# Block-sparse attention and a two-layer MLP: dense masked attention replaced by attention on gathered key and value blocks

## The chip, the cores and the metric

The kernel runs on one core of a Trainium2 chip. The metric is the device time of one execution in microseconds (us). Of the kernel before, three runs were timed; their median is 1000.07 us.

## The reference

Attention over 4 batches, 8 heads, 768 positions and head size 64, with a mask by blocks of 32 positions (24 blocks). A query block sees its neighbours, itself, the first and the last block, and three sampled blocks; the first and the last query block see everything. The result, as 3072 tokens of 512 numbers, goes through two weight matrices with a gate between them.

```python
    scores = scale * np.matmul(q, k.transpose(0, 1, 3, 2))
    mask = np.abs(blk_i - blk_j) <= window
    mask = mask | (blk_i == 0) | (blk_j == 0) | (blk_i == n_blocks - 1) | (blk_j == n_blocks - 1)
    for qb in range(n_blocks):
        for kb in sampled_blocks[qb]:
            mask[qb * block:(qb + 1) * block, kb * block:(kb + 1) * block] = True
    scores = np.where(mask, scores, -1000000000.0)
    scores = scores - np.max(scores, axis=-1, keepdims=True)
    attn = np.exp(scores)
    attn = attn / (np.sum(attn, axis=-1, keepdims=True) + 1e-09)
    return np.matmul(attn, v).astype(np.float32)
...
    h = x @ w_in
    relu6 = np.clip(h + 3.0, 0.0, 6.0)
    g = h * relu6 / 6.0
    return (g @ w_out).astype(np.float32)
```

The weights arrive as float64 and the sampled blocks as int64; both are read as pairs of 32-bit words. The inner size of the MLP is 2048.

## The kernel before

**Attention.** A unit (class `Unit`, L539) is one batch, one head and one half of the queries (384): 64 units. All 768 keys are used. To keep float32 accuracy with matmuls in the rounded format fp32r, `qh`, `ql`, `kh`, `kl` (L611 to L626) split queries and keys into a rounded high part and a low part that lie above each other on the 128 partitions. `m` (L630) makes a first product of 6 matmuls only to find the row maxima, which `r` and `fin` (L639, L645) reduce by key blocks with the mask added; `s` (L663) makes the scores a second time, keys on the output's partitions, with 12 matmuls of 384 columns, of which 6 add mask and maximum through extra rows (`KB`, `QB`). `e` is the exponential, `av` (L688) the product with the values in plain float32: from unit 12 on 6 matmuls, each on one 64-column half of the array. `suma` to `sumc` and `dm` (L722) make the denominators, which go through DRAM to be inverted and spread (`rg`, `rc`, `rs`, `rb`). `ux` (L761) splits the result into high and low parts.

**MLP.** A step (class `Step`, L774) is one unit of 384 tokens and 256 of the 2048 inner columns: 8 token units of 8 steps, 64 steps. `h` (L823) issues 24 matmuls of 384 columns in fp32r (high by high, low by high, high by low), `ga`, `gb`, `gh`, `gl` make the gate and its two parts on ACT, DVE, ACT and POOL, and `o` (L850) issues 18 matmuls of 512 columns into three PSUM banks that collect over the 8 steps. Low parts of the weights lie in DRAM and are loaded for each step. `oc` and `od` copy and store an output tile.

**Weights.** 32 chunks of 128 x 512 (class `Weight`, L491) are loaded as words (`load`), turned into float32 by `size` and `bits`, and split by `high` and `low`.

**Order.** Every engine runs its instructions in the order in which `SCORE` (L41) names them: `u11 s_0` is operation `s(0)` of unit 11, `m` a step, `w` a weight chunk, `k0` the masks. All DMAs are issued by SP, in that order, so one that waits holds those behind it. PSUM has two tiles of two banks named `big` in turn, one bank `av`, three banks `out`. `k0 warm` issues matmuls without use while TensorE has nothing else. Nearly all instructions have line L359, that of the helper which records them.

Of the kernel before, what the change touches and what calls it, by code (L numbers as in the profile page):

```python
# [17 lines left out]
P = 128  # L21
# [3 lines left out]
HALF = S // 2  # L25
NC = S // P
# [5 lines left out]
NT = HALF // P  # L32
NEG = -1000000000.0


WIDE = 12
BYDMA = 10
QUICK = "0 1 2 3 4 5 6 7 8 9 10 11 12 13 14 15 16 17 18 19 20 21 22 23 24 25 26 27 28 29 30 31"
DIRECT = "0 1 2 3"
COMPACT = "1 3 5 7 9 11"  # L40
SCORE = """  # L41
    u0 loadq loadk; k0 samp table ind ident; u0 loadv; w0 load; w2 load; u1 loadv; u0 qh qb ql kh; k0 index; u1 loadq;
    k0 allow_0 allow_1 warm_09 warm_11; u0 m_0; k0 allow_2; u0 m_1; k0 allow_3 indc; u0 r_0; k0 mq kb_0; w0 size; u0
    r_1; k0 rows; w2 size; k0 identc mqc; u0 kl m_2; k0 qb_00; u0 r_2; k0 qb_11; u1 qh qb; w0 bits_0; u1 loadk; k0
    qb_01; w0 bits_1; k0 qb_10; w0 bits_2; u0 fin_0; w0 high; w1 load; k0 kb_1; u0 fin_1; k0 warm_29 warm_39; u0 mt
    qm; w0 low; k0 warm_41; u0 s_0; u1 ql; w0 save; u0 s_1; w2 bits_0; u2 loadq; u0 e_0; w2 bits_1; u1 kh; u0 av_0; w2
    bits_2; u0 e_1; u1 kl; w3 load; u1 m_0; w2 high; u0 s_2; u1 r_0; w1 size; u0 av_1; w2 low; u2 loadk; u0 e_2; w1
    bits_0; w2 save; u2 qh; u1 m_1; w1 bits_1; u0 av_2; u2 qb; w1 bits_2; u1 r_1; w1 high; w5 load; u2 loadv; w3 size;
    w1 low; k0 warm_52; u1 m_2; u0 dw; u2 ql; w1 save; u0 uc; u1 r_2; u3 loadq; u2 kh; u1 fin_0; k0 warm_68; u2 m_0;
    u1 fin_1; u2 kl; u1 mt; u2 r_0; u1 qm; k0 warm_71; u1 s_0; w5 size; u2 m_1; w3 bits_0; u3 loadk; u1 e_0 s_1; w5  # L50
    bits_0 bits_1; u1 s_2 e_1; w5 bits_2; u1 av_0 e_2; u2 r_1; w4 load; w5 high; w3 bits_1; u2 m_2; u3 qh; u1 av_1; w5
    low; u3 qb; u2 r_2; w5 save; u3 kh; u1 av_2; u3 ql; u2 fin_0; u4 loadq; u3 m_0; u2 fin_1; u3 kl; u1 dw; u3 loadv;
    u2 mt; u3 r_0; u2 qm; w4 size; k0 warm_81; u2 s_0; u1 uc; w4 bits_0; u3 m_1; u4 loadk; u2 s_1 e_0; u1 rg; w3
    bits_2; u3 r_1; w6 load; w3 high; u2 s_2; m1 loadout_0; u2 e_1 av_0; w4 bits_1; u2 e_2; w3 low; u3 m_2; w4 bits_2;
    u4 qh; w3 save; u2 av_1; u4 qb; u3 r_2; w7 load; w4 high; u2 av_2; u3 fin_0; u4 kh ql; u1 rc; u5 loadq; u4 kl; u3
    fin_1; w6 size; u1 rs; u3 mt; u4 m_0 loadv; u3 qm; u4 r_0; u2 uc; u3 s_0; u2 dw; u5 loadk; u3 s_1; w6 bits_0; u3
    e_0; w6 bits_1; u4 m_1; u3 e_1 s_2; w6 bits_2; u3 av_0; u4 r_1; w8 load; w6 high; u3 e_2; w6 low; u1 rb; u4 m_2;
    u5 qh; w4 low; u3 av_1; w6 save; u5 qb; u4 r_2; w4 save; w7 size; u3 av_2; u5 kh; u4 fin_0; u5 ql; u4 fin_1; u5
    kl; u6 loadq; u5 m_0; u3 uc; u5 loadv; u4 mt; u5 r_0; u3 dw; u4 qm; u3 rg; k0 warm_93; u5 m_1; w7 bits_0; w8 size;
    u4 s_0; u6 loadk; w7 bits_1; m1 loadin_1; u4 s_1; m1 loadin_0; w8 bits_0; u4 e_0; w8 bits_1; u4 e_1 s_2; w8  # L60
    bits_2; u4 av_0; u5 r_1; u4 e_2; w10 load; u6 qh; u1 ux_0; u5 m_2; u6 qb; u4 av_1; u6 ql; u1 ux_1; u5 r_2; u7
    loadq; u6 kh; u4 av_2; u5 fin_0; w8 high; u1 ux_2; u5 fin_1; u6 kl; u3 rc; u5 mt; u3 rs; u6 m_0; u4 uc; u6 loadv;
    u5 qm; u6 r_0; w10 size; k0 warm_101; u5 s_0; u7 loadk; w7 bits_2; u4 dw; u5 s_1 e_0; w10 bits_0; w9 load; u6 m_1;
    w10 bits_1; u5 e_1 s_2; u6 r_1; u5 av_0; w7 high; w10 bits_2; u5 e_2; u3 rb; w8 low; u6 m_2; u7 qh; u5 av_1; u6
    r_2; w8 save; u7 qb; w11 load; u7 kh; u6 fin_0; u5 av_2; u7 ql; w10 high; u6 fin_1; u7 kl; u8 loadq; w9 size; u7
    m_0 loadv; u5 uc; u6 mt; u7 r_0; u6 qm; u5 dw; u8 loadk; k0 warm_111; u6 s_0; w9 bits_0; u5 rg; w7 low; u6 s_1
    e_0; u3 ux_0; w7 save; u7 m_1; u6 e_1 s_2; w10 low; u6 av_0; u3 ux_1; w9 bits_1; w10 save; u6 e_2; w9 bits_2; u6
    av_1; u8 qh; u7 r_1; w12 load; u8 qb kh; u3 ux_2; u6 av_2; u8 ql; w9 high; m1 loadout_1; u5 rc; u8 kl; u5 rs; w11
    size; u7 m_2; u9 loadq; u8 loadv; u6 uc; u7 r_2; u6 dw; u9 loadk; u7 fin_0; k0 warm_124; u8 m_0; u7 fin_1; w11
    bits_0; u7 mt qm; u8 r_0; w12 size; k0 warm_131; u7 s_0; w9 low; u8 m_1; u7 e_0 s_1; w11 bits_1; w9 save; u5 rb;  # L70
    u7 s_2; u8 r_1; u7 e_1 av_0; w11 bits_2; u7 e_2; w12 bits_0; w14 load; u9 kh; u8 m_2; w12 bits_1; u7 av_1; u9 qh;
    u8 r_2; u9 kl qb; w11 high; u7 av_2; u8 fin_0; u10 loadk; u8 fin_1; u9 ql; u8 mt; u7 uc; u9 loadv; w11 low; u8 qm;
    u9 m_0; u10 loadq; u7 dw; u9 m_1 r_0; w11 save; w14 size; u7 rg; u9 r_1; k0 warm_142; u8 s_0; u5 ux_0; u8 e_0 s_1;
    w12 bits_2; u5 ux_1; u8 s_2; w14 bits_0; w16 load; u8 e_1 av_0; u5 ux_2; u10 kh; w14 bits_1; u9 m_2; w14 bits_2;
    u8 e_2 av_1; u9 r_2; u10 kl; w18 load; u10 qh qb; u7 rc; u8 av_2; u7 rs; w12 high; w14 high; u9 fin_0; u11 loadk;
    u9 fin_1; u10 ql; u9 mt; u8 uc; u10 loadv; w12 low; u10 m_0; u11 loadq; u9 qm; u8 dw; u9 s_0; u10 r_0; w12 save;
    w16 size; w14 low; u9 s_1 e_0; w16 bits_0; w14 save; u9 e_1 s_2; w16 bits_1; u7 rb; u9 av_0; w18 size; w16 bits_2;
    u9 e_2; w18 bits_0; w13 load; w18 bits_1; u10 m_1; u11 kh; u10 m_2; w18 bits_2; u9 av_1; u11 qh; u10 r_1; u11 kl;
    w15 load; w18 high; u9 av_2; u11 qb; u10 r_2; w16 high; w18 low; u12 loadk; u9 uc; u11 loadv; u7 ux_0; w18 save;
# [858 lines left out]
```

## Time and profile before

| | us |
|---|---|
| timed runs | 1004.21, 1000.07, 997.81 |
| median | 1000.07 |
| profiled execution, first to last instruction (span) | 995.7 |
| TensorE matmul busy (PE) | 961.6 |
| VectorE (DVE) busy | 639.3 |
| ScalarE (ACT) busy | 471.5 |
| GpSimd (POOL) busy | 250.3 |

The profile shows one execution. The page gives its span and no separate time for what lies around it; the median of the timed runs is 4.4 us above the span. PE stands for matmuls, PEld for the weight loads that run beside them, SPq for SyncE as the issuer of DMAs. A float32 matmul is recorded as two instructions, an fp32r matmul as one. A matmul's recorded duration contains its latency, so a stream of them is read from start to start, and the last column of the timeline counts merged instructions.

### The profile page before, as it was taken

The page shows a single profiled execution, that of the slowest core. Times are in us where ns is not written, and L with a number is a line of the kernel's source. Part 1 is how long each engine was busy: PE and PEld are TensorE (multiplying, and loading weights), DVE is VectorE, ACT ScalarE, POOL GpSimd, SP SyncE. Part 2 cuts the span into 40 slices and gives each one's busy share as a digit, 9 for nine tenths or more (in the row PEclk, how much of TensorE's full clock was granted, in tenths as well). Part 3 has the DMA queues.
Part 4 walks back from the last instruction along what each step waited for, and adds up shares of the span by engine and source line. Part 5 has one row for each costly group of instructions (what it writes and reads, how often), then busy time and mean ns, then how long its engine had stood idle before and what let it go on. Part 6 is the DMA issues. An engine that isn't in the chain of part 4 may idle for free.

```text
span 995.7 us, 13391 instructions
## 1 busy us (share of the span) xinstructions
PE 961.6 (97%) x4821; PEld 780.2 (78%) x4821; DVE 639.3 (64%) x900; ACT 471.5 (47%) x712; POOL 250.3 (25%) x149
## 2 busy tenths in 40 slices
PE   8888999999999999999999999999999999999997
PEld 7666776788687888878878778887888777878886
DVE  5787898976767655676666674665766675752111
ACT  5786756563435344444453454444354443432121
POOL 3221222223314122222322233122222213302221
PEclk8999999999999999999999999999999999999999
DMA  6676887665444454435444455454543444414442
GB/s 197 202 240 183 259 290 246 191 213 163 135 131 137 134 154 144 151 103 162 151 144 140 122 161 166 123 158 127 176 147 108 147 131 139 144 49 146 140 119 72
DMA packets 103702, 155.49 MB, mean 156 GB/s; under 512 B 32819, under 2 KB 51891, under 8 KB 103636
## 3 DMA queue, kind: packets, MB, share of 16 engines
q1 hardware_dynamic: 103636, 154.64, 51.1%
q8 instruction: 38, 0.62, 0.3%
q14 instruction: 28, 0.23, 0.1%
HBM read 139.63 MB, written 14.78 MB: 155 GB/s over the span
## 4 chain that ended last, share of the span: by engine, by line
PE 82%; DVE 10%; ACT 2%; DMA 2%; issue 2%; POOL 0%; SPq 0%; DVEq 0%; ACTq 0%
PE big L359 44%; PE out L359 26%; PE av L359 12%; DVE bm L359 3%; DVE xhl L359 2%; DVE acc L359 2%; DVE QA L359 2%; ACT pr L359 1%; DMA wout_lo<-xhl 1%; DMA wraw<-w_out 1%; ACT xhl L359 1%; DMA win_lo<-xhl 0%; DVE wraw L359 0%; ACT qb L359 0%; DVE uu L359 0%
## 5 line engine op out<-in xcount | busy, mean ns | idle before, releaser
L359 PE MATMUL big<-xhl,win_hi 128*128 128x384 f32 x1024 | 264.7, 340 | 0.7 <-DVE bm L359 0.7
L359 POOL TENSOR_TENSOR glo<-g,ghi 128x768 fp32r<-128x768 f32 x64 | 119.8, 1873 | 432.0 <-ACT ghi L359 420.6
L359 ACT ACTIVATE pr<-big 128x768 f32<-128x768 f32 x192 | 153.1, 809 | 101.6 <-PE big L359 100.9
L359 POOL TENSOR_TENSOR kb<-kraw,KA 64x768 fp32r<-64x768 f32 x64 | 124.5, 1945 | 299.6 <-ACT KA L359 242.1
L359 PEld LDWEIGHTS big<-xhl,win_hi 128*128 128x128 f32 x1024 | 184.5, 188 | 14.1 <-issue 7.3
L359 DVE TENSOR_REDUCE bm<-big 128x24 f32<-128x768 f32 x168 | 158.2, 953 | 55.9 <-PE big L359 54.3
L359 PE MATMUL big<-xhl,wlo_in 128*128 128x384 f32 x512 | 172.5, 337 | 0.0
L359 PE MATMUL av<-pr,vo 128*64 128x384 f32 (+1 forms) x768 | 162.7, 493 | 0.2 <-ACT pr L359 0.2
L359 PE MATMUL out<-wout_hi,ghi 128*128 128x512 f32 x384 | 153.3, 399 | 4.7 <-DVE wraw L359 4.7
L359 PE MATMUL out<-wout_hi,glo 128*128 128x512 f32 x384 | 152.1, 396 | 0.0
L359 PE MATMUL out<-wlo_out,ghi 128*128 128x512 f32 x384 | 150.4, 392 | 0.0
L359 PE MATMUL big<-QA,KA 128*128 128x384 f32 x384 | 137.1, 357 | 2.2 <-DVE bm L359 0.8
L359 PE MATMUL big<-qb,kb 97*128 97x384 f32 x384 | 131.2, 342 | 0.6 <-ACT qb L359 0.4
L359 DVE SCALAR_TENSOR_TENSOR g<-g,big 128x768 f32<-128x768 f32 x64 | 60.8, 950 | 110.7 <-ACT g L359 110.4
L359 ACT ACTIVATE g<-big,half_b 128x768 f32<-128x768 f32 x64 | 57.7, 901 | 144.6 <-PE big L359 129.0
L359 PEld LDWEIGHTS av<-pr,vo 128*64 128x64 f32 (+1 forms) x768 | 67.0, 146 | 65.3 <-issue 49.4
L359 PE MATMUL big<-KA,QA 128*128 128x384 f32 x336 | 92.3, 366 | 9.0 <-DVE QA L359 4.1
L359 PEld LDWEIGHTS big<-KA,QA 128*128 128x128 f32 x336 | 74.5, 255 | 31.6 <-issue 8.6
L359 DVE TENSOR_TENSOR acc<-pr 128x768 f32<-128x768 f32 x52 | 54.2, 1042 | 68.2 <-ACT pr L359 68.0
L359 PEld LDWEIGHTS big<-xhl,wlo_in 128*128 128x128 f32 x512 | 96.2, 188 | 0.0
L359 PEld LDWEIGHTS big<-QA,KA 128*128 128x128 f32 x384 | 73.2, 191 | 21.7 <-ACT pr L359 6.1
L359 ACT CAST ghi<-g 128x768 fp32r<-128x768 f32 x64 | 53.3, 833 | 73.4 <-DVE g L359 50.9
(66 smaller groups left out, 1005.3 us busy)
## 6 DMA issues: line engine op xcount, KB each, us to landing
wlo_out<-wout_lo SPq DMA_DIRECT2D x126, 256.0 KB, 2.9
wlo_in<-win_lo SPq DMA_DIRECT2D x126, 256.0 KB, 2.9
kraw<-kT SPq DMA_DIRECT2D x64, 384.0 KB, 3.8
qraw<-qT SPq DMA_DIRECT2D x64, 192.0 KB, 2.8
vo<-vP SPq DMA_DIRECT2D x64, 192.0 KB, 2.8
wraw<-w_in SPq DMA_DIRECT2D x16, 512.0 KB, 3.9
wraw<-w_out SPq DMA_DIRECT2D x16, 512.0 KB, 4.4
rec<-rec SPq DMA_DIRECT2D x64, 96.0 KB, 3.5
```

The source lines that it names most:

```text
L359: return lambda *a, **k: tc.keep_in_program_order(op(*a, **k))
```

## The change

The kernel is rewritten around the attention; MLP and weight arithmetic are the same instructions in another order.

- The 24 query blocks of a batch form six groups of four: five of inner blocks, and one (g = 5) of blocks 21, 22, 0 and 23. A group has all 8 heads; three groups make one token unit of 384. `GROUPS` is their order.
- `Pair` holds keys and values of two neighbouring query blocks: for each, 8 slots of 32 positions. `kw` and `vw` load the three neighbour blocks with one DMA, `kg` and `vg` the first and last block, `kr` and `vr` the three sampled blocks of each, with one DMA per block whose address comes from a register. `registers` issues one load of six values into registers of SP; before each such DMA stands one register instruction (ISA). There are 44 pairs and three buffers, so pair n waits for the readers of pair n - 3. Positions that appear twice are masked by pointing their values, with their column of ones, at a block of zeros (index 0 of `vG`).
- `Job` (44 of them) is 128 query rows by 4 heads: `s` 16 plain float32 matmuls on 64 rows x 32 columns of the array with 256 columns moving, `mx` the maximum and its scale, `e` four exponentials of 256 columns, `t` 8 transposes, `cv` or `ca` the copy out of PSUM on DVE or ACT, `av` 32 float32 matmuls on 32 columns of the array with 65 columns moving (the 65th gives the denominator), `dn` and `ml` the division, `x` 2 transposes back, `xh` and `xl` the split.
- `Dense` (8) does blocks 0 and 23 on all keys in the same manner with 64-column tiles.
- Before `m0` stand six jobs; the other jobs and the dense ones stand between the MLP steps up to `m55`. The order's first steps carry the 32 weight chunks. No `warm`.

```diff
-        def m(self, t):
...
-            for j in range(2):
-                pe.matmul(ps[:, j, :HALF], lhsT=self.QA[:, t:HALF:NT], rhs=self.KA[:, j * HALF:(j + 1) * HALF], start=True, stop=True)
...
+KP = [const.tile([P, 2, 8, HP * BLK], F32, name=f"kp{i}") for i in range(3)]
+VP = [const.tile([P, 2, 2, VR], F32, name=f"vp{i}") for i in range(3)]
...
+    def registers(row):
+        loads, values = nc.values_load_multi_w_load_instructions(
+            row, engines=[mybir.EngineType.SP], min_val=0, max_val=NB - 1,
+            skip_runtime_bounds_check_because="sampled blocks are numbers of blocks")
...
+        def kr(self):
+            at = NR * self.i
+            for n, r in enumerate(registers(index.raw[:, 2 * at:2 * at + 4 * NR:2])):
+                dma.dma_start(out=self.k[:, n // NR, 3 + n % NR], in_=kG[self.b][:, bass.ds(r * (HP * BLK), HP * BLK)])
...
+        def s(self):
+            self.ps = big_tile()
+            q = self.group.q
+            for x in range(2):
+                for t in range(4):
+                    pair, j = self.tile(t)
+                    hp = self.hp(t, x)
+                    for y in range(2):
+                        half = slice(64 * y, 64 * y + 64)
+                        pe.matmul(self.ps[32 * t:32 * t + 32, y, 256 * x:256 * x + 256],
+                                  lhsT=q[half, hp, 32 * (j if self.few else t):][:, :32],
+                                  rhs=pair.k[half, j, :, BLK * hp:BLK * hp + BLK], start=True, stop=True)
...
+        def t(self, y):
+            if y == 0:
+                self.pt = big_tile()
+            for c in range(4):
+                pe.transpose(self.pt[:, y, c * P:c * P + P], self.pr[y][:, c * P:c * P + P], ident)
...
+        def av(self, y):
+            if y == 0:
+                self.us = small_tile()
+            for x in range(2):
+                for c in range(2):
+                    for t in range(4):
+                        pair, j = self.tile(t)
+                        h = 2 * self.hp(t, x) + y
+                        at = (2 * x + y) * VW
+                        pe.matmul(self.us[32 * t:32 * t + 32, at:at + VW], lhsT=self.prT[y][:, (2 * x + c) * P + 32 * t:][:, :32],
+                                  rhs=pair.v[:, j, c, h * VW:h * VW + VW], start=c == 0, stop=c == 1)
...
+    k0 samp table ident; q0 load; p0 kw; p1 kw; p0 kg; k0 index; p1 kg; p0 kr; p1 kr; p0 vw; p1 vw; p0 vg; p1 vg; p0
...
+    m16 h_01; j17 e_10 e_11; m16 h_11; m18 loadin_0; j17 t_0; m16 ga; m18 loadin_1; j17 t_1 cv_0; m15 o_00; j17 ca_1;
```

TensorE, in the middle of the MLP stage before: scores (`big<-KA,QA`) and values (`av`) of a unit between pieces of `h` (`xhl,win_hi`) and `o`.

```order
L359 MATMUL out<-wout_hi,ghi 128x512
L359 MATMUL out<-wlo_out,ghi 128x512
L359 MATMUL out<-wout_hi,glo 128x512
L359 MATMUL big<-KA,QA 128x384 x2
L359 MATMUL av<-pr,vo_120 64x384 x6
L359 MATMUL big<-KA,QA 128x384 x2
```

TensorE now, in a step that carries a job: 8 transposes (`ident,p`), one piece of `o`, then `av` (32 matmuls in rows of two); row names are out<-in and the output's partitions x columns.

```order
L286 MATMUL big<-ident,p 128x128 x8
L286 MATMUL out<-wout_hi,ghi 128x512
L286 MATMUL out<-wlo_out,ghi 128x512
L286 MATMUL out<-wout_hi,glo 128x512
L286 MATMUL small<-vp_109,pT 32x65 x2
L286 MATMUL small<-vp_110,pT 32x65 x2
```

What moved: a job's 58 matmuls stand in one step, its `s` before five pieces of `o`, its `av` after the sixth; before, a unit's 24 stood in groups over several steps.

SP at the start before: queries, keys, values and the first weights.

```order
L359 DMA qraw<-qT 128x384
L359 DMA kraw<-kT 128x768
L359 DMA samp<-sampled 24x6
L359 DMA tab<-table 24x48
L359 DMA pr<-krows 33x768
L359 DMA tmp<-ident 128x128
L359 DMA vo_120<-vP 128x6x64
L359 DMA wraw<-w_in 128x1024 x2
```

SP at the start now: the first query group, the neighbour and end blocks of two pairs, then a register load and the first gathered blocks.

```order
L286 DMA q<-qT 128x512
L286 DMA kp_106<-kG 128x2x384
L286 DMA kp_107<-kG 128x2x384
L286 DMA kp_106<-kG 128x2x128 x2
L286 DMA kp_107<-kG 128x2x128 x2
L342 TENSOR_LOAD raw
L286 ISA
L286 DMA kp_106<-kG 128x128
L286 ISA
L286 DMA kp_106<-kG 128x128
```

What moved: the weight loads stand behind the gathers of the first six pairs, and SP has 1043 DMAs, 88 register loads and 528 register instructions in all.

## Rows read from the trace of the kernel before

**Rows 1.** The page: span, busy time, and TensorE and its clock in 40 slices.

```profile
span 995.7 us, 13391 instructions
PE 961.6 (97%) x4821; PEld 780.2 (78%) x4821; DVE 639.3 (64%) x900; ACT 471.5 (47%) x712; POOL 250.3 (25%) x149
PE   8888999999999999999999999999999999999997
PEclk8999999999999999999999999999999999999999
```

**Rows 2.** The chain from 900 us on: start us, us, what, count.

```profile
910.30 4.20 PE big L359 x24
...
937.57 6.29 PE out L359 x27
```

**Rows 3.** Tiles xhl and mneg on PE: duration ns min/median/max, first and last start us.

```profile
L359 PE MATMUL big<-xhl,win_hi x1024: 331/337/632, 116.1 to 976.9; 128*128 128x384 f32 x171
...
L359 PE MATMUL big<-ident,mneg x30: 218/223/516, 16.5 to 105.2; 128*2 128x128 f32 x30
```

**Rows 4.** Groups by form on PE and PEld: busy us, mean ns of one, idle before.

```profile
L359 PE MATMUL out<-wout_hi,ghi 128*128 128x512 f32 x384 | 153.3, 399 | 4.7 <-DVE wraw L359 4.7
L359 PE MATMUL av<-pr,vo 128*64 128x384 f32 x624 | 112.1, 495 | 0.0
L359 PE MATMUL av<-pr,vo 128*128 128x384 f32 x144 | 50.6, 487 | 0.2 <-ACT pr L359 0.2
L359 PE MATMUL big<-acc,ones 128*32 128x384 f32 x104 | 13.5, 498 | 0.5 <-DVE acc L359 0.5
L359 PEld LDWEIGHTS big<-acc,ones 128*32 128x32 f32 x104 | 2.4, 108 | 8.9 <-issue 4.4 <-DVE acc L359 3.1 <-DVE bm L359 0.6
L359 PEld LDWEIGHTS big<-ident,mneg 128*2 128x2 f32 x30 | 2.2, 83 | 3.3 <-issue 2.6
```

**Rows 5.** Timeline of PE and PEld at three places: start us, us, instruction, count.

```profile
7.34 2.39 PE L359 MATMUL out<-mval,pr 24*128 24x24 f32 x12 [1.01 <-DVE mval L359]
...
16.45 0.34 PE L359 MATMUL big<-ident,mneg 128*2 128x128 f32 x3
...
209.46 0.16 PEld L359 LDWEIGHTS big<-acc,ones 128*32 128x32 f32 x8 [0.25 <-ACT pr L359]
...
209.47 0.85 PE L359 MATMUL big<-acc,ones 128*32 128x384 f32 x8
210.25 2.16 PE L359 MATMUL av<-pr,vo 128*64 128x384 f32 x12
```

**Rows 6.** Groups by form on DVE, ACT and POOL.

```profile
L359 DVE TENSOR_REDUCE bm<-big 128x24 f32<-128x768 f32 x168 | 158.2, 953 | 55.9 <-PE big L359 54.3
L359 ACT ACTIVATE pr<-big 128x768 f32<-128x768 f32 x192 | 153.1, 809 | 101.6 <-PE big L359 100.9
L359 ACT ACTIVATE QA<-qraw 128x384 fp32r<-128x384 f32 x64 | 33.4, 522 | 13.5 <-PE big L359 12.3 <-DMA qraw<-qT 1.2
L359 DVE COPY wraw<-out 128x512 f32<-128x512 f32 x24 | 16.2, 687 | 22.8 <-PE out L359 22.8
```

**Rows 7.** Timeline of SP at the start and at 400 us: start us, us, instruction, count.

```profile
0.75 0.39 SPq L359 DMA_DIRECT2D qraw<-qT  x1
1.19 0.42 SPq L359 DMA_DIRECT2D kraw<-kT  x1
...
400.06 2.54 SPq L359 DMA_DIRECT2D rec<-rec  x4
```

**Rows 8.** DMA issues: KB each, median us from issue to landing.

```profile
qraw<-qT SPq DMA_DIRECT2D x64, 192.0 KB, 2.8
```

**Rows 9.** Stretches: length, busy us (count) of PE, PEld, DVE, ACT, POOL, clock, DMA share, GB/s.

```profile
5.60:9.00 3.40, 2.39 (x14) 2.13 (x13) 3.26 (x5) 0.00 (x0) 3.23 (x4) 1.00 0.95 299
9.00:15.80 6.80, 6.80 (x23) 6.30 (x23) 4.25 (x10) 4.72 (x9) 1.27 (x2) 0.50 0.51 150
500.00:600.00 100.00, 100.00 (x522) 80.20 (x515) 69.58 (x94) 47.39 (x71) 26.92 (x14) 1.00 0.49 147
```

More of the change, by code (lines that the diff above doesn't have):

```diff
@@ new lines, with blocks, plan @@
+"""
+def blocks(g):
+    return [4 * g + 1 + i for i in range(4)] if g < 5 else [LAST - 1, LAST, 0, NB - 1]
+def plan():
+    pairs, jobs, dense = [], [], []
+    for n, (b, g) in enumerate(GROUPS):
+        mine = []
+        for i in range(2 if g < 5 else 1):
+            mine.append(len(pairs))
+            pairs.append((b, blocks(g)[2 * i]))
+        for u in range(2 if g < 5 else 1):
+            jobs.append((n, u, mine))
+        if g == 5:
+            for u in range(2):
+                dense.append((n, u))
+    return pairs, jobs, dense
@@ L340, in big_tile, with small_tile @@
         return big.tile([P, 2, 512], F32, name="big")
-    units = [(b, h, hf) for b in range(B) for hf in range(2) for h in range(H)]
-    win_hi = const.tile([P, NF, DM], F32R, name="win_hi")
-    wout_hi = const.tile([P, NF, DM], F32R, name="wout_hi")
-    win_lo_d = [dram.tile([P, DM], F32, name=f"win_lo{i}") for i in range(NF)]
-    wout_lo_d = [dram.tile([P, DM], F32, name=f"wout_lo{i}") for i in range(NF)]
+    def small_tile():
+        return small.tile([P, 512], F32, name="small")
     class Ordered:
@@ L863, in od @@
+            dve.tensor_copy(out=self.ot[t], in_=OUT[:, t])
         def od(self, t):
-            if self.fp == NFP - 1:
-                r0 = self.b * S + self.hf * HALF + t * P
-                dma.dma_start(out=out[r0:r0 + P], in_=self.ot[t])
-    NU = len(units)
-    masks = Masks()
-    units = [Unit(n, *u) for n, u in enumerate(units)]
-    for x in units:
-        x.last = units[x.n // 4 * 4 + 3]
-    steps = [Step(n, n // NFP // 2, n // NFP % 2, n % NFP) for n in range(NU)]
+            dma.dma_start(out=out[self.unit, t], in_=self.ot[t])
@@ L875, in fused_kernel @@
+    pair_list, job_list, dense_list = plan()
+    index = Index()
+    pairings = [Pair(n, *x) for n, x in enumerate(pair_list)]
+    groups = [Group(n, *x) for n, x in enumerate(GROUPS)]
+    jobs = [Job(n, *x) for n, x in enumerate(job_list)]
+    dense = [Dense(n, *x) for n, x in enumerate(dense_list)]
+    steps = [Step(n) for n in range(NU * NFP)]
     weights = []
-    quick = [int(x) for x in QUICK.split()]
-    direct = [int(x) for x in DIRECT.split()]
-    compact = [int(x) for x in COMPACT.split()]
@@ L896, in fused_kernel @@
-    if "warm" in SCORE:
-        masks.do("heat")
-    set_constants()
-    play(SCORE)
+        weights.append(Weight(w_in[f], win_hi[:, f], win_lo_d[f], f, "in"))
+        weights.append(Weight(w_out[f], wout_hi[:, f], wout_lo_d[f], f, "out"))
+    works = {"k": [index], "p": pairings, "q": groups, "j": jobs, "d": dense, "m": steps, "w": weights}
+    nc.gpsimd.memset(half_b, 0.5)
+    for phrase in SCORE.split(";"):
+        who, *ops = phrase.split()
+        for op in ops:
+            works[who[0]][int(who[1:])].do(op)
```

1132 lines of the change are left out of this document (455 added, 677 removed), and 11 rows, old and new, of the table NEEDS.

## The prediction

> **What bounds the kernel now.** I read the page first: TensorE is busy for 97% of a span of 995.7 us, at full clock in nearly every slice [rows 1], so the question is what its time consists of. The chain near the end, where hardly any attention is left, gives the MLP alone: 24 matmuls of 384 columns in 4.20 us and 27 of 512 columns in 6.29 us, 0.233 us each [rows 2]. A step (24 and 18) costs 4.20 + 4.19 = 8.39 us and 64 steps 537 us. The reader is to see there that nothing lies between the matmuls. The view of the tile xhl gives the first `h` at 116.1 us [rows 3]: before that there are ten units and weight work. Of a unit, the 18 fp32r matmuls cost 18 x 0.175 = 3.15 us, and `av` (12 instructions, two at a time, in 2.16 us of which the last 0.495 is latency: (2.16 - 0.495) / 5 = 0.333 us a round [rows 4, 5]) 6 x 0.333 = 2.0 us: 5.15 us. So 116.1 + 537 + 54 x 5.15 + 13 denominators of 0.78 [rows 5] = 941 us of 995.7. The 55 us left are waits and changes between forms of matmul. The kernel is bound by TensorE, and in the first 116 us by getting started.
>
> **What the change removes.** All 64 units go, about 54 x 5.15 = 278 us of TensorE time behind the 116 us, with the dummy matmuls and the denominators' way through DRAM. The 537 us of the MLP stay, the same matmuls.
>
> **What a job costs on TensorE.** No row before shows a matmul on 64 rows x 32 columns, or one of 65 columns, so each part gets two ends.
>
> `s`: 32 instructions of 256 columns. The denominators are the nearest row: float32, weights of 32 columns, four column tiles at once. Their eight instructions and the change to the next form take 210.25 - 209.47 = 0.78 us [rows 5], two rounds of 0.333 and 0.11 us lost, against 0.351 us for one instruction alone (50.6 us / 144 [rows 4]). So four column tiles run side by side at full rate. A round of 256 columns is 0.222 us; eight rounds are 1.8 us, or four, 0.9 us, if the two row halves overlap too, which no row shows. They write different PSUM banks, so I take 1.1 us.
>
> The Trainium skill, page "TensorEngine Tiling (Array Packing)", section Tiling Modes, lists 64x32 as eight independent tiles; by it the lower end holds, 0.2 us a job less than I take, and no run here shows it yet.
>
> `t`: 8 transposes of 128 columns. As two instructions each at 0.351 / 3 = 0.117 us they take 1.9 us. Ends: half of that (0.95), if a transpose is one instruction; and 16 x 0.2 = 3.2 us, if the weight load of 128 columns isn't hidden, as where twelve matmuls with 24 moving columns took 2.39 us [rows 5]. I take 1.9: rows with more moving columns hide the load.
>
> `av`: 64 instructions of 65 columns, 16 rounds of four tiles. Streaming is 0.333 x 65 / 384 = 0.056 us a round; a weight load of 32 columns takes 25 ns more than one of 2 (108 against 83 [rows 4]), and with so short a stream I count it as not hidden, 0.027 us. So 16 x 0.083 = 1.3 us; ends 0.9 us and 3.8 us (below, the first rival). `x`: 4 x 0.117 = 0.5 us. Four changes of form at 0.11 us: 0.45 us. A job is 1.1 + 1.9 + 1.3 + 0.5 + 0.45 = 5.25 us, with ends 3.5 and 10.
>
> 38 jobs stand behind `m0`: 200 us. A dense item by the same rates is 1.6 (`s`) + 2.8 (24 transpose instructions) + 2.0 (48 instructions, two tiles) + 0.65 = 7.0 us; eight are 56 us. This is 256 us where 278 went: on TensorE the attention gets hardly cheaper. The float32 passes and the transposes eat nearly all that the smaller block set saves.
>
> **The start.** SP needs, before the first token unit is complete, 102 DMAs, 12 register loads and 72 register instructions (six pairs of 14 DMAs, 12 for end blocks, six others). SP starts one DMA each 0.42 to 0.44 us in the first microseconds [rows 7]: 102 x 0.42 = 43 us. Register loads and register instructions appear nowhere in the trace; bounds for a load are 0.1 us (a short instruction) and 2.3 us (nearly a small DMA's way, 2.8 us [rows 8]); I take 1.0 us, 12 us in all. For a register instruction, between nothing and 0.1 us, I take 0.06 us: 4 us. With 2.8 us to land [rows 8] and about 8 us for the last two jobs' chain the first `h` starts at 43 + 12 + 4 + 3 + 8 = 70 us, 46 us earlier than now; ends 52 and 104. This is where the gain lies, since the first steps also carry the weights that now fill the first 116 us and more.
>
> **What must stay hidden.** In the first five steps SP issues 140 DMAs, 12 loads and 72 register instructions, 75 us, against 5 x (8.39 + 5.25) = 68 us on TensorE: 7 us late. Later a step's most urgent pair is one load, six register instructions and seven DMAs, 4.3 us, and 2.8 us to land, behind the job that frees its buffer; a step is 13.6 us, so it is covered. If it were not, a job would wait, its `s` standing before five pieces of `o`, and all of TensorE with it. Within a step, the maximum takes 0.953 x 1024 / 768 = 1.3 us, the four exponentials 0.235 + 256 x 0.75 ns = 0.43 us each (a line through 0.522 at 384 and 0.809 at 768 columns [rows 6]): 3.2 us with the hand-overs, against 3.5 us of `o`. That margin is thin; each 0.1 us over it costs 4 us in all. The copies (0.69 us [rows 6]) lie beside a piece of `o` (0.70) and the second four transposes. DVE and ACT have about 4.5 us of work in a step of 13.6 and don't bind.
>
> **The sum.** 70 (start) + 537 + 200 + 56 + 7 (SP in the first steps) + 3 (end) + 39 for waits that nothing above names, = 912 us of span. The 39 are the 55 us of before without 11 for changes of form, which the jobs contain now, and without the 4.7 us in which `out` waited for its tile to be copied [rows 4], since the copies now stand half a step ahead of the next unit's `o`. The median of the runs lies 4.4 us above the profiled span, so I say 915 us.
>
> **The rivals.**
> *TensorE is held by the number of small matmuls, not by their columns (slower than before).* Three matmuls with weights of only two columns start 60 ns apart ((0.34 - 0.22) / 2, with 0.22 us the median of one [rows 3, 5]). If each instruction of `s` and `av` costs 60 ns whatever its size, they take 96 x 0.06 = 5.8 us a job for my 2.4, which is +3.4 x 38 = 129 us, and 0.9 us on each dense item: 915 + 129 + 7 = 1051 us. Against it: the denominators' eight weight loads start (0.16 - 0.108) / 7 = 7 ns apart [rows 4, 5], though that is a short burst out of a filled queue. From 50 ns an instruction on, the gain is gone.
>
> The Trainium skill, page "TensorE: Matmul & The Clock Gate", Part 1, "Wait — 56ns, not 53.3ns?", gives a floor of about 25 ns from start to start, which would leave my sum within 12 us, and about 62 ns per matmul where a sequencer decodes them in software, which is this rival; the 7 ns above speaks for the first, but no run here has a long enough row of small matmuls.
>
> *The clock falls in jobs.* Between 9.0 and 15.8 us it was 0.50 of full speed, 1.2 GHz, behind a stretch in which PE was busy for 2.39 of 3.40 us, partly with matmuls of 24 columns [rows 9]. If jobs run at that level, their 4.8 us of streaming double: 915 + 38 x 4.8 + 8 x 6 = 1145 us. Against it: with 8.4 us of dense matmuls in each step the stretch resembles 500 to 600 us, at 1.00 [rows 9].
>
> *SP binds.* If a gathered DMA costs 0.635 us, as four in a row did at 400 us [rows 7], and a load 2.3 us, the start grows by 72 x 0.215 + 12 x 1.3 = 31 us, the first five steps by about the same: 977 us. Later steps keep slack.
>
> **How the numbers follow.** My forecast gets 0.64, spread over 820 to 980 by the ends of start, transposes and `s` (52 us at the start and 4.0 us a job with half the waits give about 820). SP binding gets 0.12, small matmuls 0.15, the clock 0.05; 0.04 is for a mixture that ends at about the time of before. Below 1%, some 10 us, a measurement of this kernel can't tell from no change. Faster: 0.64 + 0.12 and a little of the mixture, 0.77; same 0.05; slower 0.18. The range goes from 820 to 1035 us.
>
> **What would show it.** Right: the first `win_hi` matmul at about 70 us; gaps of under 0.1 us between matmuls of a step; starts of consecutive steps 13 to 14 us apart where a job stands in them and 8.4 us where not; clock 1.00 from 100 us on; `small<-vp,pT` busy for 1.3 us a job. Wrong: that group at 3 us or more (first rival), a clock of 0.5 in steps with a job (second), TensorE waiting for DMAs into `kp` or `vp` behind SP's register loads (third), or a chain of maximum and exponentials that outlasts five pieces of `o`.

## The result and the profile after

The changed kernel takes 986.81 us (median of three runs, 986.03 to 989.37) against 1000.07 us before: a ratio of 0.9873, with a 95% interval of 0.983 to 0.9916. The forecast was 915 us, with a range from 820 to 1035.

The head of the page after, with TensorE's slices and clock as in [rows 1], and the chain that ended last, by engine:

```profile
span 985.0 us, 20294 instructions
PE 827.3 (84%) x7968; PEld 656.8 (67%) x7968; DVE 342.2 (35%) x590; ACT 274.1 (28%) x496; POOL 152.2 (15%) x93
...
PE   3567776687899799977998989977999888999997
...
PEclk9756877878799799988999989988999999999999
...
PE 54%; SPq 21%; DMA 14%; issue 5%; DVE 5%; ACT 2%; POOL 0%; ACTq 0%; DVEq 0%; POOLq 0%
```

The same chain by engine in the kernel before:

```profile
PE 82%; DVE 10%; ACT 2%; DMA 2%; issue 2%; POOL 0%; SPq 0%; DVEq 0%; ACTq 0%
```

TensorE's busy time fell by 134 us, but the span by 11 only. Before, TensorE was busy for 97% of the span; now it is for 84%. Its share of the chain fell from 82% to 54%, and 21% of the chain is now SyncE (SP, in its rows SPq), issuing DMAs, which had no share before. What that costs is the subject of the experiments.

The first piece of `h` starts at 90.2 us; in [rows 3] it was 116.1:

```profile
L286 PE MATMUL big<-x,win_hi x1024: 331/338/689, 90.2 to 969.2; 128*128 128x384 f32 x171
```

The stretches after, cut at the starts of step 0, step 8 and step 55 (columns as in [rows 9]: length, busy us of PE, PEld, DVE, ACT, POOL, clock, DMA share, GB/s):

```profile
0.00:90.20 90.20, 48.96 (x669) 25.87 (x669) 30.76 (x64) 18.26 (x40) 3.56 (x7) 0.75 0.64 180
90.20:256.40 166.20, 119.88 (x1111) 95.57 (x1109) 105.52 (x154) 69.66 (x128) 43.94 (x29) 0.80 0.85 258
256.40:896.70 640.30, 577.71 (x5755) 464.89 (x5756) 190.53 (x352) 170.28 (x310) 88.05 (x48) 0.96 0.62 186
896.70:985.00 88.30, 80.80 (x439) 70.47 (x437) 15.40 (x21) 15.90 (x19) 16.61 (x9) 0.99 0.37 110
```

The start is 26 us shorter than before. After it TensorE idles for 46 us in steps 0 to 7, which carry the weights, and for 63 us in steps 8 to 54, which carry jobs; in the last stretch, from step 55 on, it idles for 7.5 us.

What a job costs, from the timeline of PE in a step without a wait (start us, us, instruction, count):

```profile
499.78 1.09 PE L286 MATMUL big<-kp,q 64*32 64x256 f32 x32
500.80 0.62 PE L286 MATMUL big<-x,win_hi 128*128 128x384 f32 x2
...
504.15 1.09 PE L286 MATMUL big<-ident,p 128*128 128x128 f32 x8
505.00 0.60 PE L286 MATMUL big<-x,win_hi 128*128 128x384 f32 x2
...
506.24 1.12 PE L286 MATMUL small<-vp,pT 128*32 128x65 f32 x64
507.28 0.50 PE L286 MATMUL out<-wout_hi,ghi 128*128 128x512 f32 x1
...
511.86 1.09 PE L286 MATMUL big<-kp,q 64*32 64x256 f32 x32
```

From start to start `s` takes 500.80 - 499.78 = 1.02 us, the eight transposes 0.85, `av` 1.04. The whole step, from one `s` to the next, is 12.08 us; less the 8.39 us of the MLP, a job costs 3.69 us; what is not in these three groups lies in the two transposes back and in the changes between forms.

SP at the start and in the middle (start us, us, instruction, count; register loads and register instructions are inside the merged rows):

```profile
2.32 12.11 SPq L286 DMA_DIRECT2D kp<-kG  x18
14.49 12.69 SPq L286 DMA_DIRECT2D vp<-vG  x18
...
73.20 0.42 SPq L286 DMA_DIRECT2D stage<-w_in  x1
...
532.42 4.88 SPq L286 DMA_DIRECT2D kp<-kG  x7
537.39 0.38 SPq L286 DMA_DIRECT2D q<-qT  x1
537.86 0.38 SPq L286 DMA_DIRECT2D wlo_out<-wout_lo  x1
538.30 5.56 SPq L286 DMA_DIRECT2D kp<-kG  x7
543.95 5.26 SPq L286 DMA_DIRECT2D vp<-vG  x7
549.27 0.42 SPq L286 DMA_DIRECT2D wlo_out<-wout_lo  x1
549.75 5.71 SPq L286 DMA_DIRECT2D vp<-vG  x7
555.56 0.84 SPq L286 DMA_DIRECT2D wlo_out<-wout_lo  x2
556.45 1.84 SPq L286 DMA_DIRECT2D wlo_in<-win_lo  x4
```

And the `s` on PE just before this row:

```profile
531.29 1.09 PE L286 MATMUL big<-kp,q 64*32 64x256 f32 x32
```

SP begins at 532.42 us, when the `s` that started at 531.29 has ended and a K buffer is free, and works without a pause to past 555 us on one group: two pairs, each with a K part and a V part of 5 to 6 us. Two pairs take 23 us, and two steps with a job take 24.2. The weight loads of the steps stand between and behind them: with those behind, SP's row ends at 558.3 us, 25.9 us after its start and longer than the two steps that it feeds.

What SP spends on them, by line (duration ns min/median/max, first and last start):

```profile
L342 SPq TENSOR_LOAD <-raw x44: 1266/1276/2819, 5.4 to 828.1; - x44
L342 SPq TENSOR_LOAD <-vblk x44: 1267/1279/2642, 18.0 to 839.1; - x44
...
L286 SPq FUSED_REGOPS  x528: 37/46/56, 6.9 to 844.2; - x176
...
L286 SPq MOVE vp<-vG x264: 29/29/38, 19.4 to 844.3; - x132
```

A register load of six values takes 1.28 us (1.33 from start to start). A gathered DMA comes with two register instructions (46 and 29 ns; the listing ahead of the prediction shows one) and takes 0.526 us from start to start, a plain one 0.474. All of SP's issuing is about 88 x 1.33 + 528 x 0.526 + 515 x 0.474 = 639 us of 985: not a full engine, but in order, and in bursts.

What TensorE waits for after (us in all, times, longest us):

```profile
PE out L286 <- DMA wlo_out<-wout_lo: 28.8, 13, 5.7
PE big L286 <- ACT p L286: 23.2, 12, 6.0
PE big L286 <- DMA kp<-kG: 17.5, 9, 10.3
PE small L286 <- DVE xq L286: 17.3, 8, 6.2
PE small L286 <- DMA stage<-vD: 15.0, 3, 5.2
```

The largest wait is not for a gathered block at all: it is for the low parts of the output weights, 256 KB loads that stand in SP's queue behind the gathers. Of the 23.2 us for `p`, the exponentials, 9.8 lie in the start and 12.3 in steps 0 to 7.

### The profile page after: what moved, and what is told of

Read it like the earlier page. It is cut to its first block, busy times and chain, and to the rows that moved or that the text cites. A ratio compares the mean times of both kernels' runs of the same rounds, so it can differ in the third digit from the quotient of the medians.

```text
span 985.0 us, 20294 instructions
## 1 busy us (share of the span) xinstructions
PE 827.3 (84%) x7968; PEld 656.8 (67%) x7968; DVE 342.2 (35%) x590; ACT 274.1 (28%) x496; POOL 152.2 (15%) x93
## 2 busy tenths in 40 slices
DMA packets 134898, 187.71 MB, mean 191 GB/s; under 512 B 16659, under 2 KB 69012, under 8 KB 134804
## 4 chain that ended last, share of the span: by engine, by line
PE 54%; SPq 21%; DMA 14%; issue 5%; DVE 5%; ACT 2%; POOL 0%; ACTq 0%; DVEq 0%; POOLq 0%
PE big L286 28%; PE out L286 20%; SPq L286 16%; PE small L286 5%; SPq L342 5%; DMA wlo_out<-wout_lo 4%; DMA stage<-w_out 3%; DMA stage<-w_in 3%; DVE wf L286 2%; DMA out_dram<-wf 1%; DVE pT L286 1%; DMA stage<-vD 1%; DMA kp<-kG 1%; DMA wlo_in<-win_lo 1%; ACT wf L286 1%
## 5 line engine op out<-in xcount | busy, mean ns | idle before, releaser
L286 PE MATMUL big<-x,win_hi 128*128 128x384 f32 x1024 | 282.4, 358 | 14.8 <-DVE g L286 14.6
L286 PEld LDWEIGHTS big<-x,win_hi 128*128 128x128 f32 x1024 | 189.9, 198 | 27.4 <-ACT win_hi L286 9.5
L286 PE MATMUL big<-x,wlo_in 128*128 128x384 f32 x512 | 178.8, 349 | 5.1 <-DMA wlo_in<-win_lo 3.5
L286 PE MATMUL out<-wlo_out,ghi 128*128 128x512 f32 x384 | 156.8, 408 | 28.8 <-DMA wlo_out<-wout_lo 28.8
L286 PE MATMUL out<-wout_hi,ghi 128*128 128x512 f32 x384 | 166.2, 433 | 12.1 <-DVE wf L286 10.3
L286 DVE TENSOR_REDUCE m<-big 128x4 f32<-128x1024 f32 (+1 forms) x60 | 68.8, 1151 | 190.2 <-PE big L286 190.2
L286 ACT ACTIVATE p<-big,m 128x256 f32<-128x256 f32 (+1 forms) x208 | 85.8, 491 | 153.4 <-DVE m L286 147.8
L286 PEld LDWEIGHTS out<-wout_hi,ghi 128*128 128x128 f32 x384 | 75.0, 195 | 48.1 <-issue 16.9
L286 PEld LDWEIGHTS out<-wlo_out,ghi 128*128 128x128 f32 x384 | 75.5, 197 | 46.1 <-DMA wlo_out<-wout_lo 34.8
L286 PEld LDWEIGHTS big<-x,wlo_in 128*128 128x128 f32 x512 | 100.5, 196 | 7.3 <-DMA wlo_in<-win_lo 4.7
L286 PE MATMUL big<-ident,p 128*128 128x128 f32 x448 | 70.1, 302 | 26.2 <-ACT p L286 23.2
L286 PEld LDWEIGHTS out<-wout_hi,glo 128*128 128x128 f32 x384 | 75.1, 196 | 20.1 <-POOL glo L286 3.0
```

The source lines that it names most:

```text
L286: return lambda *a, **k: tc.keep_in_program_order(op(*a, **k))
```

## The experiments

The theories in the texts on record: **A**, SP's serial work on the gathers (loads, register instructions, issues) binds, all through; **B**, the DMA engines or their bytes bind; **C**, TensorE's lower clock stretches the steps with weights. Each experiment was timed in four runs, the changed kernel in three; times are medians, ratios are to the kernel before, timed again beside each group of experiments, with 95% intervals. The stages are read from one profiled execution of each kernel (that of e4 was its fastest, 975.4 us): the start (to the first `win_hi`), steps 0 to 7, and steps 8 to 54; the rest is 88 us in every kernel.

| kernel | us | ratio | start | steps 0 to 7 | steps 8 to 54 |
|---|---|---|---|---|---|
| after | 986.8 | 0.9873 [0.983, 0.9916] | 90.2 | 166.2 | 640.3 |
| e1 constant addresses | 911.7 | 0.911 [0.908, 0.914] | 75.5 | 154.2 | 595.2 |
| e2 same bytes, fewer DMAs | 868.6 | 0.8695 [0.8676, 0.8715] | 72.4 | 131.9 | 574.3 |
| e3 raw weights on ACT's queue | 982.2 | 0.9816 [0.9783, 0.9848] | 92.2 | 162.7 | 638.5 |
| e4 all weight and output DMAs on ACT's queue | 981.8 | 0.9836 [0.9801, 0.9871] | 91.1 | 162.3 | 631.9 |
| e5 one load a pair | 946.6 | 0.9475 [0.9448, 0.9501] | 84.6 | 161.2 | 608.8 |
| e6 e5 and e4 together | 954.9 | 0.954 [0.9497, 0.9583] | 88.4 | 159.6 | 619.7 |
| e7 no sampled blocks | 856.2 | 0.8564 [0.8538, 0.859] | 69.4 | 132.7 | 564.1 |
| e8 dummy matmuls | 983.2 | 0.9827 [0.9785, 0.987] | 90.3 | 163.7 | 640.2 |
| e9 V part on GpSimd | 903.7 | 0.9017 [0.897, 0.9064] | 81.1 | 146.7 | 586.0 |
| e10 V part on ACT | 1039.1 | 1.0352 [1.0286, 1.0417] | 94.8 | 180.3 | 676.6 |
| e11 one load a group | 941.7 | 0.9412 [0.9361, 0.9462] | 83.0 | 156.0 | 611.3 |

**e1: constant block numbers.** No register loads and no register instructions; the same number of DMAs, of the same size. The kernel leaves out the choice of the sampled blocks and computes another mask.

```diff
-            for n, r in enumerate(registers(index.raw[:, 2 * at:2 * at + 4 * NR:2])):
-                dma.dma_start(..., in_=kG[self.b][:, bass.ds(r * (HP * BLK), HP * BLK)])
+            for n in range(2 * NR):
+                r = (5 * self.i + 7 * n) % NB
+                dma.dma_start(..., in_=kG[self.b][:, r * (HP * BLK):(r + 1) * (HP * BLK)])
```

> The sampled blocks are replaced by constant block numbers, so the 88 register loads and 528 register moves go, while DMAs, bytes and all else stay; the output is that of another mask. Theory A (SP's issue is late, and each pair's gather is slow on SP): a pair's nine-DMA key part takes 5 us instead of 6.4, the eight steps with weights shrink from 166 us to about 145, the first win_hi comes at about 80 instead of 90 us, in all 940 to 960 us. Theory B (the DMA engines or landing times bind, not SP): unchanged, 980 to 990 us. Theory C (the granted clock of 1.2 GHz in the first 260 us binds): unchanged within 1%.

Measured: 911.7 us, 75 us less than the changed kernel and below the 940 to 960 us of theory A. The work that left SP is 88 x 1.33 + 528 x 0.052 = 144 us; about half of it showed. Its chain by engine:

```profile
PE 68%; DMA 17%; DVE 6%; SPq 5%; issue 2%; ACT 2%; ACTq 0%; DVEq 0%
```

And TensorE's wait for `wlo_out` (us, times, longest us):

```profile
PE out L286 <- DMA wlo_out<-wout_lo: 4.3, 4, 2.4
```

SP's share of the chain went from 21% to 5%, and that wait from 28.8 to 4.3 us, though the weight loads themselves were not touched. They had been late because they stood behind register loads and register instructions.

**e2: constant block numbers, and five DMAs a pair instead of fourteen,** with the same bytes: the three sampled blocks of both query blocks are neighbours and come with one DMA for K and two for V.

```diff
+            src = bass.AP(src.tensor, src.offset + r * HP * BLK, [list(src.ap[0]), [3 * HP * BLK, 2], [1, 3 * HP * BLK]])
+            dma.dma_start(out=self.k[:, :, 3:6].rearrange("p j s n -> p j (s n)"), in_=src)
```

> As the run with constant block numbers, and three neighbouring blocks come with one DMA: per pair 5 issues of SP instead of 14, no register work, the same bytes; the output is that of another mask. Theory A: SP has slack everywhere; first win_hi at 55 to 65 us, the eight steps with weights 120 to 130 us, no wait for wlo_out or vD behind the gathers, 860 to 890 us in all, and the clock recovers by itself. Theory B: at most 1% faster, since bytes and engines are as loaded. Theory C: the clock stays at 1.2 GHz for about half of the first 260 us and the time stays above 960 us.

Measured: 868.6 us, another 43 below e1. Steps 0 to 7 of this kernel:

```profile
72.40:204.30 131.90, 105.55 (x1113) 82.99 (x1108) 108.57 (x158) 69.22 (x129) 42.99 (x29) 0.91 0.98 317
```

The same bytes go through in 132 us, at 317 GB/s for the 258 of the changed kernel, so their number is not what held these steps at 166. But fewer DMAs are also fewer packets (106,022 for 134,898): whether the 43 us are SP's issuing alone, or in part the DMA engines' work on small packets, this edit doesn't separate.

**e3 and e4: other DMAs leave SP.** In e3 the weight words and the stores of their low parts, in e4 also the low parts' loads of all steps and the output stores (312 DMAs) go to ACT's queue.

```diff
-            dma.dma_start(out=self.raw, in_=self.src.bitcast(I32).rearrange("p (n t) -> p n t", t=2))
+            dma2.dma_start(out=self.raw, in_=self.src.bitcast(I32).rearrange("p (n t) -> p n t", t=2))
```

> Only the loads and saves of the 32 weight chunks are issued by ACT instead of SP (64 DMAs, about 22 us of ACT's time); all is computed as before. Theory A: the weight loads no longer stand behind the gathers; ACT's 50 us of waiting for stage shrink, and the eight steps with weights go from 166 to about 135 us: 950 to 960 us. Theory B or C: unchanged, or slower by ACT's waits in its queue: 985 to 1000 us.

> All DMAs of weights, MLP loads and outputs (312) are issued by ACT; SP keeps queries, keys, values and registers; all is computed as before. Theory A: as the run with the weights alone, and the waits for wlo_out (28 us) and vD (15 us) later in the kernel go too, less what ACT's own order costs (312 issues of 0.35 us on an engine busy for 28%): 910 to 940 us. Theory B or C: unchanged or slower, 985 to 1010 us.

Measured: 982.2 and 981.8 us. Both ratios' intervals overlap that of the changed kernel, where theory A had said 950 to 960 and 910 to 940 us. That is not what A had led to expect; the waits of e4 show what SP still holds up:

```profile
PE small L286 <- DMA stage<-vD: 31.8, 3, 12.2
PE small L286 <- DMA vp<-vG: 31.5, 22, 4.1
```

The wait for `wlo_out` is gone, and waits for `vp` (4.9 us in the changed kernel) and `vD` (15.0) have taken its place. SP's burst for a group is still as long as two steps (496.8 to 520.8 us in e4), and whatever is last in it is late. In these runs only taking work out of the burst itself helped.

**e5: one register load a pair.** The K part uses the same six registers as the V part. Blocks that appear twice are then read as block 0 in K, which their zeroed values mask.

```diff
-            for n, r in enumerate(registers(index.raw[:, 2 * at:2 * at + 4 * NR:2])):
+            self.regs = registers(index.v[:, at:at + 2 * NR])
+            for n, r in enumerate(self.regs):
...
-            for n, r in enumerate(registers(index.v[:, at:at + 2 * NR])):
+            for n, r in enumerate(self.regs):
```

> A pair's six block numbers are loaded into SP's registers once instead of twice (keys and values use the same six numbers; where the number is 0 for a position that appears twice, the values are zeros and the keys are those of block 0, so the result is the same). That takes 44 of the 88 register loads, 44 x 1.28 = 56 us, off SP. If the register loads are what held the gathers: about half of what constant addresses gave (75 us), 945 to 960 us. If the gain of constant addresses came from the 528 register moves and slower DMAs with a register address instead: 975 to 987 us.

Measured: 946.6 us. 44 loads, 58 us of SP, gave 40 us.

**e6: e5 with the 312 other DMAs on ACT's queue.**

> One register load per pair, and the 312 DMAs of weights, MLP loads and outputs on ACT. If SP's time is the bound, both reliefs add: 920 to 940 us. If moving DMAs gave so little because ACT's own order delays them (or because the weight stage is held by the DMA engines), then about as the one-load kernel alone, 940 to 960 us.

Measured: 954.9 us, not better than e5, as the second of the two expectations said. ACT issues in its own order, and its own work now waits behind loads of `wlo_in` and `wlo_out` in its queue, waits that e5 doesn't have:

```profile
ACT p L286 <- DMA wlo_in<-win_lo: 14.5, 9, 1.8
ACT x L286 <- DMA wlo_out<-wout_lo: 11.8, 4, 3.9
```

**e7: no sampled blocks at all.** Neither registers nor gathers; the slots of the sampled blocks hold constants, so the kernel computes attention on the window and end blocks with constant rows. All TensorE work stays.

```diff
-            for n, r in enumerate(registers(index.raw[:, 2 * at:2 * at + 4 * NR:2])):
-                dma.dma_start(...)
+            pass
```

> All DMAs and register work for sampled blocks are left out (528 DMAs, 34 MB); the buffers' slots hold a constant, and the jobs compute as before; the output is that of constant sampled blocks. With SP free and the bytes less: if the DMA engines (busy for 0.85 in the weight stage) held that stage, its eight steps fall clearly below the 132 us of the kernel with few DMAs, to 110 to 120 us, and the whole to 845 to 855 us. If they did not, the stage stays at 128 to 134 us and the whole at 860 to 870 us, and the rest is the order of ACT, DVE and TensorE.

Measured: 856.2 us. Chain by engine:

```profile
PE 80%; DVE 11%; issue 2%; ACT 2%; POOL 2%; DMA 2%; SPq 0%; ACTq 0%; POOLq 0%
```

This is the kernel with the gathers taken away, bytes and all. Against it the changed kernel loses 90.2 - 69.4 = 21 us at the start, 166.2 - 132.7 = 34 us in steps 0 to 7 and 640.3 - 564.1 = 76 us in steps 8 to 54: 131 us. Steps 0 to 7 of this kernel:

```profile
69.40:202.10 132.70, 105.60 (x1116) 82.73 (x1109) 108.79 (x158) 69.30 (x129) 43.15 (x29) 0.91 0.83 261
```

They take the same 132 us here and in e2, with a DMA share of 0.83 here and 0.98 there, so the DMA engines don't hold these 132 us. For the 34 us above them, B falls in the greater part: e9 below does all the gathers, with the same bytes and nearly as many packets (130,675), in 146.7 us. What is left, 14 us, is not separated.

**e8: eight dummy matmuls before the transposes of jobs 6 to 13.**

```diff
+                for i in range(8 if 6 <= self.n < 14 else 0):
+                    pe.matmul(self.pt[:, 0, :P], lhsT=ident, rhs=ident, start=True, stop=True)
```

> Before the transposes of jobs 6 to 13, where TensorE waits for exponentials, stand 8 float32 matmuls without use (about 2 us each time at full clock). Theory C (the clock of 1.2 GHz costs the weight stage much): the clock of 90 to 256 us rises from 0.80 to over 0.9 and the time falls by 15 us or more, to 970 us or less. Theory A (it waits for SP and DMAs): the clock rises and the time stays within 980 to 995 us.

Measured: 983.2 us; the intervals of the two ratios lie over each other. Steps 0 to 7 of this kernel:

```profile
90.30:254.00 163.70, 125.68 (x1238) 104.21 (x1236) 106.41 (x154) 69.65 (x127) 44.05 (x29) 0.89 0.85 261
```

The granted clock rose from 0.80 to 0.89, about half of what was missing, and the stage got 2.5 us shorter of the 34 that it loses to the gathers. This alone doesn't settle C, since the dummies take time too: from the start of each row of them to the first transpose behind it, 18 us in all, where the changed kernel waited for 8 us before these transposes. e7 and e2 settle more: at 0.91, without a dummy, they need 132 us for these steps, and this kernel at 0.89 needs 163.7, of which the dummies explain 18 at most. So the lower clock goes with the waits, and C falls as the main cause; the clock's own share isn't isolated.

**e9, e10, e11: ways to make the burst shorter,** all on top of e5. e9 lets GpSimd load its own registers and issue the V part's 264 gathers, e10 lets ACT do the same, e11 loads the 12 values of a group's two pairs at once.

```diff
-            for n, r in enumerate(self.regs):
+            for n, r in enumerate(registers(index.v[:, at:at + 2 * NR], mybir.EngineType.Pool)):
...
-                dma.dma_start(out=self.v[s % 4 * BLK:(s % 4 + 1) * BLK, n // NR, s // 4], in_=src)
+                pool.dma_start(out=self.v[s % 4 * BLK:(s % 4 + 1) * BLK, n // NR, s // 4], in_=src)
```

> The kernel with one register load a pair, but GpSimd loads its own registers and issues the V part's 264 gathered DMAs; SP keeps the K part. Theory A (the serial issue work of one queue binds): SP loses 264 x 0.526 = 139 us of work, GpSimd has room (152 of 985 us busy); removing all 528 gathers (336 us of SP with the loads) took 946.6 to 856.2, so 139/336 of 90 gives about 909 us, range 890 to 930; TensorE's waits for vp nearly gone. Rival (an engine that issues DMAs in order holds its own work): a DMA that waits for its buffer holds glo behind it on GpSimd, TensorE waits for glo, and the time is 940 to 980 us.

Measured: 903.7 us, the best version with the whole computation: 83 us under the changed kernel and 96 under the 1000.07 of the kernel before. GpSimd's two main groups:

```profile
L286 POOL DMA_DIRECT2D vp<-vG x264 | 131.8, 499 | 139.3 <-PE small L286 76.0 <-issue 43.7 <-DMA vp<-vG 3.2
L286 POOL TENSOR_TENSOR glo<-g,ghi 128x768 fp32r<-128x768 f32 x64 | 117.9, 1842 | 402.6 <-ACT ghi L286 400.6 <-PE small L286 1.9
```

A gather is recorded with 0.5 us on GpSimd, which has that time in the later steps. TensorE's waits for GpSimd, in this kernel and, last, in the changed one:

```profile
PE out L286 <- POOL glo L286: 0.2, 1, 0.2
PE big L286 <- POOL wlo_in L286: 14.0, 5, 5.3
...
PE big L286 <- POOL wlo_in L286: 1.6, 2, 0.9
```

For `glo` the rival's price did not come. It came in steps 0 to 7, where GpSimd also makes the low parts of the weights: `wlo_in` stands behind gathers (one was started at 116.66 us, right behind six gathers from 113.12 us on, and TensorE waited 5.3 us for it), 14 us in all. They are part of what e9 still has above e7.

> The same with the V part's registers and gathered DMAs on ACT instead of GpSimd. Theory A, if ACT's own work left room: about 909 us as well. Rival (order on the issuing engine, as in the two kernels with the weight loads on ACT): ACT, 274 us busy and on the path of each job's exponentials, carries 264 x about 0.5 = 130 us more between them, and the time is 935 to 965 us, with TensorE waiting for p and ghi more than before.

Measured: 1039.1 us, slower than before the change, and far above both expectations. The same gathers on ACT hold the MLP and the jobs:

```profile
ACT p L286 <- DMA vp<-vG: 84.4, 12, 10.1
...
ACT g L286 <- DMA vp<-vG: 43.3, 7, 8.5
ACT ghi L286 <- DMA vp<-vG: 42.4, 6, 8.9
```

The exponentials, the gate and its high part stood behind the gathers for 170 us. The queue's engine decides, not the number of DMAs on it.

> One register load for the two pairs of a group (12 values), 24 loads in all instead of 44, everything else as in the kernel with one load a pair. Theory A: 20 x 1.33 = 27 us less on SP; by the rate of that kernel (58 us of loads gave 40 us) 18 us, so about 928 us (920 to 937). Rival (only the loads that stood between the K and V part of one pair mattered): 943 to 949 us.

Measured: 941.7 us, 5 us under e5, with intervals that overlap, where 18 us were expected. The row of the loads tells why:

```profile
L342 SPq TENSOR_LOAD <-vblk x24: 1262/2476/3054, 5.4 to 782.8; - x24
```

A load of 12 values takes 2.48 us, twice that of 6: the price is by value, some 0.2 us each. The 24 loads cost 20 x 2.48 + 4 x 1.28 = 55 us, as 44 x 1.28 = 56 did. The expectation had priced an instruction where it had to price values.

## Why the prediction was wrong in size

**The start: right in direction, 20 us too short.** The start got shorter by 26 us, to 90.2. Forecast was 70 us, 46 less than before, from SP's 102 DMAs and 12 loads. SP issued the first weight load, behind all of them, at 73.2 us instead of 59 (43 + 12 + 4), as a gathered DMA is 0.526 us, not 0.42, and a load 1.33, not 1.0; waits for buffers lie in it as well. But without any gather the start still takes 69.4 us (e7): two limits stand beside each other, SP's row of issues and the serial chains of six jobs, at a clock of 0.70 there (0 to 69 us). The prediction added a tail of 11 us to the one and did not see the other; the tail was 17 us (73.2 to 90.2).

**The job, too dear.** Taken 5.25 us, measured 3.69. Transposes are one instruction each (448 = 44 jobs x 8 and 8 dense items x 12), 0.85 us and not 1.9; `s` 1.02 for 1.1; `av` 1.04 for 1.3; two transposes back 0.14 for 0.5. So 38 x 1.56 = 59 us less. By the Trainium skill, page "TensorEngine Tiling (Array Packing)", section Tiling Modes, 64x32 gives eight independent tiles; the trace agrees: eight rounds of 0.222 us would be 1.78 us, and `s` took 1.02. With the gathers taken away (e7) the whole comes to a span of 854, less than the 905 that the sum holds without its 7 us for SP: the part of the sum without SP was too high, by about what the jobs were too dear.

**The step that failed: "What must stay hidden", and with it the sum's 7 us.** It priced SP at 7 us in the first five steps and nothing later. The runs show 110 us behind the start, 34 in steps 0 to 7 and 76 in steps 8 to 54 (and 21 in the start, which the sum priced by itself). That is what the gathers cost in all, against e7; of the 131 us, e1 shows 75 to be the register work on SP alone, and e9 shows 83 to go when the second load and the V part leave SP's queue, with the same bytes. The rest, in which bytes and packets may have a part, is not separated. Three things were wrong in the step. A step's "most urgent pair" was one load, six register instructions and seven DMAs, 4.3 us: that is the K part alone, and it took 4.9 to 5.6 us. The V part, with its own load, takes as long and stands in the same queue, as do the step's four weight loads (1.9 us). And with three buffers and two pairs in use by both jobs of a group, the next group's pairs cannot be loaded one by one; they come in a burst of 23 us, 25.9 with the weight loads behind it, as long as two steps. So "later steps are covered" was a comparison of a part of the queue's work with a whole step; the work to be compared was all that one engine issues between two uses of a buffer. That most of it can be hidden is shown by e2 (574 us in steps 8 to 54 with five DMAs a pair) and e9 (586, in two queues), against 564 without any gather. No run gave the pairs a fourth buffer or SP's queue another order, so how much of the wait a longer lead would have hidden stays open.

**How the total came about.** 915, 20 us more for the start, 59 less for the jobs and 110 in place of 7 for SP make 979 of the measured 986.8 us. So the cheap jobs hid half of the miss: that the total stayed within 72 us of the forecast is luck.

**The 39 us for other waits** were about right: with the gathers gone (e7) PE is idle for 854.3 - 777.6 = 77 us, 31 of them in the start (37.8 us busy of 69); 46 are left. The thin margin of maximum and exponentials held behind step 7: about 1 us of the 23.2 us that the changed kernel's TensorE waits for `p` lies there.

**The rivals.** *SP binds* had the mechanism, at 977 us, with a load at 2.3 us and a gather at 0.635 (measured 1.33 and 0.526). Its total came close to 986.8 by luck, two errors that cancel, since it kept the dear jobs; and its claim that later steps keep slack, on which its size rested, is the largest miss: 76 us. *The number of small matmuls*: 64 instructions of `av` take 1.04 us, 16 ns each, for the 60 ns of this rival; it falls. The Trainium skill, page "TensorE: Matmul & The Clock Gate", Part 1, "Wait — 56ns, not 53.3ns?", has about 62 ns for matmuls decoded in software, and no row here shows that. The prediction takes a floor of about 25 ns between starts from the same section; the 16 ns measured here, with the instructions going to four tiles in turn, lie under it, and the measurement decides. *The clock*: 0.80 in steps 0 to 7, against the forecast's 1.00 from 100 us on, 0.96 later and 1.00 in a step with a job and no wait (501.0 to 512.9 us); 0.91 in steps 0 to 7 of e2 and e7, where the waits for gathers are gone.

**What stays open.** Steps 0 to 7 take 132 us even without the gathers, where 8 x (8.39 + 3.69) = 97 us of TensorE work stand. VectorE is busy for 83 of 100 us there (90 to 190 us, e7), which points to the weights' arithmetic and its order; no run changed that. In e9, steps 22 and 38, which carry dense items, are still 24 us long for 16 in e7. The clock's own share of steps 0 to 7, the part of bytes and packets in e2's gain, and the effect of more buffers are not measured.

## What to carry to other kernels

When a change trades arithmetic for gathers by register, price the issuing engine like any other: add up every load (by value), register instruction and DMA that it issues between two uses of a buffer, and compare that with the time in which TensorE uses up the buffer, not the most urgent piece of it with one step. If it doesn't fit, first remove instructions (share registers, merge DMAs), then give part of them to the queue of an engine with little in-order work of its own; here the same move to ACT, which the jobs wait for, took 15% longer than to GpSimd, and even GpSimd made TensorE wait where it had weights to prepare. A wait for one tensor can be the debt of others ahead of it in the queue: here the largest wait was for weight loads that the change had not made more or larger.

## What the runs showed of the hardware that was not expected

- A register load on SP takes 1.28 us for six values and 2.48 us for twelve; on GpSimd 1.39 us for six.
- A DMA with a register address takes SP 0.526 us from start to start against 0.474 for a plain one: the register is cheap, the load of it is not.
- 32 float32 matmuls on 64 x 32 tiles with 256 columns take 1.02 us at full clock, and 64 on 32-column tiles with 65 columns 1.04 us, 16 ns each (counted as recorded: two instructions a matmul).
- A float32 transpose of 128 x 128 is recorded as one instruction, 0.107 us from start to start, where a float32 matmul is two.
